# A linear-attention and feed-forward kernel: weights asked for ahead of stores, one visit moved behind two inner products, and banks marked without a full fill

## The chip, the cores and the metric

The kernel runs on one core of a Trainium2 chip. The metric is the time of one execution on the device in microseconds (us), taken over several runs. A core has five engines with instruction queues of their own: PE (matrix products, its weight loads shown apart as PEld), DVE (vector work), ACT (copies and activation functions), POOL (a second, slower vector engine) and SP, which here issues the transfers (DMA). PE writes into eight PSUM banks of 128 partitions by 512 fp32 columns; DVE and ACT read them. Each engine takes its own instructions in order and waits for others by semaphores.

## The reference

Two blocks, one after the other, in fp32. The first is a recurrence with decay for each of 4 sequences and 8 heads of width 64, over 768 steps:

```
state = gamma * state + k[t] (outer) v[t]
y[t]  = scale * q[t] @ state
```

Its outputs, as 3072 tokens of 512, go through a feed-forward block with a leaky function between:

```
h = x @ w_in                 # 512 -> 2048
out = maximum(0.01*h, h) @ w_out   # 2048 -> 512
```

## The kernel before, in words

**Chunks and visits.** The 768 steps are cut into 6 chunks of 128 (`c` from 0 to 5). A chunk of all four sequences (`b` from 0 to 3) is 512 tokens. What the kernel does for a chunk's recurrence is called a *visit*, two sequences at a time. It has products of queries and state (`reads`, line 190), products of masked scores and values (`last_values` L225, `first_values` L214), the sums for the next state (`state`, L240), and ahead of these the *scores* (`scores_to`, L157), products of keys and queries, which DVE multiplies by a causal mask (`masked_apart`, L323) into `am`. DVE then takes the tokens into `x` (`tokens_taken`, L270 and L273) and updates the states (L283, L287). `between`, a tiny POOL instruction (L194), only keeps an order among PE's products. POOL also multiplies the values of coming chunks by their decay (`decay_v`, L127), when they have been loaded (`ahead` L111, `load_kv` L307).

**Feed-forward in units.** The width of 2048 is cut into four units (`u`). For a chunk and a unit there is a hidden product and an output product. Both use Strassen's scheme in Winograd's form: 2 by 2 blocks, seven products M1 to M7 in place of eight, paid for by sums and differences on DVE (`differences`, L489; `plus`, L486). `seven` (L542) issues the seven products into four banks called A, B, C and D. Some banks are shared: M1 is copied by ACT from one bank to another (L635), and a later product is added by PE on top of the copy.

**The first part** does chunks 0 and 1, unit by unit, while the weights arrive. Dictionaries named `hidden_more` and `output_more` say what other work is put after which of the seven products: `s2` means after the third. In the output of chunk 0 and unit 3, written `(0, 3)`, a visit of chunk 2 stands at `s2`, and at `s3` the differences for the last output of chunk 1, those of chunk 2, and the loads of the heads of chunk 3. Sums of the hidden weights are kept in DRAM (`keep_unit`, L909: `kept<-w`, `kept<-sums`).

**The second part** does chunks 2 to 5, 16 units numbered `n`. Here the hidden product has two levels of the scheme. Its weights are streamed from `kept` for each unit by `load_unit`: group 0 into `wa` (L1012, L1013), group 1 into `wb` (L1015, L1016). `inner(n, group)` (L1046) makes the seven inner products of the group into banks 0 to 3: 28 in number times the blocks of the group, four for group 0 and three for group 1, 128 columns each. M1 is copied by ACT into bank 3 (L1050), and M6 is added there without the start flag[...]. ACT copies M5, M4, M6 and M2 out (L1052 to L1058), DVE adds M3 and M7. `outer(n, group)` then adds the inner results to `g` on DVE, and ACT applies the leaky function (L1081). For a unit the order on PE is inner of the next unit's group 0, four products of the output, inner of group 1, three products.

**The seam.** Between the parts the last output of chunk 1 (`last`) is issued in pieces, and between these stand the scores of chunk 3 for sequences 0 and 1, `inner(0, 0)`, the first `joint_visit` of chunk 3 and `inner(0, 1)`. `joint_visit` uses banks 4 to 7 for its sums, and banks 0 to 3 for the scores of the visit that follows. With `scores_first` it computes and masks those scores before its own work. The scores are written with the start flag in each product[...]; `fill(3)` (L575) writes all 512 columns of bank 3 with a product of bf16 values[...], and ACT's copy overwrites the values. It can be issued only after DVE has read the masked scores from the bank.

SP takes the issues of transfers in the order of the program. The order of the last statements before the loop is:

```
for group in range(2):
    load_unit(0, group)
...
inner(0, 0)
outer(0, 0)
products(last, 2)
xs[3] = new_x(3)
joint_visit(3, 0, (3, 2), scores_first=True)
fill(3)
inner(0, 1)
outer(0, 1)
```

Of the kernel before, what the change touches and what calls it, by code (L numbers as in the profile page):

```python
# [9 lines left out]
FP32 = mybir.dt.float32  # L10
# [8 lines left out]
C = 128  # L19
# [3 lines left out]
def kernel(  # L23
# [14 lines left out]
    nc = tc.nc  # L38
# [107 lines left out]

    NS = HP // 2 * 3 * C // 2

    def scores_to(x, ps):
        for m in range(HP // 2):  # L150
            for i in range(2):
                for late in range(2):
                    for j in range(2):
                        s, a = i ^ j, 2 * m + i
                        to = (ps[j][ts(1 - s, 64), m, 1 + s] if late else
                              ps[j][ts(s, 64), m, 0 : 2 + s : 1 + s])
                        nc.tensor.matmul(to, lhsT=x[ts(j, 64), 1, a, ts(late, 64)],  # L157
                                         rhs=x[ts(j, 64), 0, a, late * 64 :])

    turn = [0]  # L160

# [148 lines left out]

    def score_apart(c, b, banks=None):

        if banks is None:
            banks = [ffs.tile([128, HP * C], FP32, tag="ff", bufs=4, name=f"ap{j}_{c}_{b}")
                     for j in range(2)]
        banks = [ps[:, 0:NS] for ps in banks]
        scores[c, b] = [ps.rearrange("p (m n t) -> p m n t", n=3, t=C // 2) for ps in banks]
        scores_to(heads[c, b][0], scores[c, b])

    def masked_apart(c, b, j):  # L320
        if j == 0:
# [11 lines left out]
    def visit(c, b):  # L333

        for f in (reads, last_values, state, first_values):
            for i in range(2):
                f(c, b + i)
        for i in range(2):
            tokens_taken(c, b + i, xs[c][0])
        for i in range(2):  # L340
            state_taken(c, b + i, for_state(sums_at[c, b + i]))
        for i in range(2):
            heads.pop((c, b + i))

    def joint_visit(c, b, following, scores_first=False):

        both = [(c, b), (c, b + 1)]
        later = [(following[0], following[1] + i) for i in range(2)] if following else []
        for i, at in enumerate(both):
            sums_at[at] = [bank[4 + 2 * i + j].rearrange("p (a t) -> p a t", t=C)  # L350
                           for j in range(2)]
        for i, at in enumerate(later) if scores_first else ():
            score_apart(*at, banks=bank[2 * i : 2 * i + 2])
            for j in range(2):
                masked_apart(*at, j)
        for at in both:
            reads(*at)
        for at in both:
            last_values(*at)
        if c < NC - 1:  # L360
            for at in both:
                state(*at)
        else:
            for i in range(2):
                fill(4 + 2 * i, 2, start=False)
        for at in both:
            first_values(*at)
        for i, at in enumerate(later) if not scores_first else ():
            score_apart(*at, banks=bank[2 * i : 2 * i + 2])
        for j in (1, 0):  # L370
            for at in both:
                tokens_taken(*at, xs[c][0], j)
                if j == 0:
                    state_added(*at, for_state(sums_at[at]))
                    heads.pop(at)
        for at in later if not scores_first else ():
            for j in range(2):
                masked_apart(*at, j)
        for at in both:
            state_decayed(*at)  # L380
        for i in range(2):
            ahead(c + 1, b + i)
        for at in later:
            load_kv(*at)
        for at in later:
            decay_v(*at)
# [533 lines left out]
    def sums(c, group):  # L920
        return lambda: sums_of_x(c, group)

    def next_heads():
        for b in range(2):
            ahead(3, b)
            load_kv(3, b)
        for b in range(2):
            decay_v(3, b)
# [17 lines left out]
        (1, 1): dict(s6=[sum_of_unit(1, 1)]),  # L946
        (0, 2): dict(s2=[sum_of_unit(2, 1)], s5=[sum_of_unit(2, 2)]),
        (1, 2): dict(s0=[sum_of_unit(2, 3)], s1=[keep_unit(2)]),
        (0, 3): dict(s2=[lambda: visit(2, 0)],
                     s3=[lambda: differences(*parts[1][1:]), differ(2), next_heads],  # L950
                     s6=[sums(2, 0)]),
    }

# [21 lines left out]
    for u in range(NU):  # L975
# [7 lines left out]
        for c in range(2 if u < NU - 1 else 1):  # L983
            if u == 0:
# [6 lines left out]
    banks = ctx.enter_context(tc.tile_pool(name="banks", bufs=1, space=bass.MemoryType.PSUM))  # L991
    bank = [ffs.tile([128, 4 * C], FP32, tag="ff", bufs=4, name=f"bank{i}") for i in range(4)]
    bank += [banks.tile([128, 4 * C], FP32, name=f"bank{i}") for i in range(4, 8)]
    wa = work.tile([128, 7, 4, C], FP32, tag="late4", name="wa")
    wb_room = work.tile([128, 28 * C], FP32, tag="late6", name="wb")
    wb = wb_room[:, 0 : 21 * C].rearrange("p (j i n) -> p j i n", j=7, i=3)
    made_room = work.tile([128, 28, C], FP32, tag="late0", name="made")
    made_of = [made_room[:, 0:16].rearrange("p (q i) n -> p q i n", q=4),
               made_room[:, 16:28].rearrange("p (q i) n -> p q i n", q=4)]

    N2 = (NC - 2) * NU

    def at_of(n):
        return 2 + n // NU, n % NU

    def load_unit(n, group):

        if n >= N2:
            return
        u = at_of(n)[1]  # L1010
        if group == 0:
            nc.sync.dma_start(out=wa[:, :, 0:1], in_=kept[u][:, :, 0:1])  # L1012
            nc.sync.dma_start(out=wa[:, :, 1:4], in_=kept[u][:, :, 3:6])  # L1013
        else:
            nc.sync.dma_start(out=wb[:, :, 0:2], in_=kept[u][:, :, 1:3])  # L1015
            nc.sync.dma_start(out=wb[:, :, 2:3], in_=kept[u][:, :, 6:7])  # L1016

    def operands(c, group):

# [17 lines left out]
    def inner(n, group, held=False):  # L1037

        c, u = at_of(n)
        w, count = ((wa, 4), (wb, 3))[group]  # L1040
        moving = operands(c, group)
        sums = made_of[group]
        ps = [part[:, 0 : count * C].rearrange("p (i n) -> p i n", n=C) for part in bank[0:4]]
        for m, q, j, s in INNER:
            for i in range(count):
                nc.tensor.matmul(ps[q][:, i], lhsT=w[:, j, i], rhs=part_of(moving[i], s),  # L1046
                                 start=(i == 0 and m in ("M1", "M5", "M4")), stop=True,
                                 skip_group_check=True)
            if m == "M1":
                nc.scalar.copy(out=ps[3], in_=ps[0])  # L1050
            elif m == "M5":
                nc.scalar.copy(out=sums[:, 3], in_=ps[1])  # L1052
            elif m == "M4":
                nc.scalar.copy(out=sums[:, 2], in_=ps[2])
            elif m == "M6":
                nc.scalar.copy(out=sums[:, 1], in_=ps[3])
            elif m == "M2":
                nc.scalar.copy(out=sums[:, 0], in_=ps[0])  # L1058
            elif m == "M3":
                plus(sums[:, 1], sums[:, 1], ps[1])  # L1060
            elif m == "M7":
                plus(sums[:, 3], sums[:, 3], ps[3])
                plus(sums[:, 2], sums[:, 2], ps[3])
        if not held:
            load_unit(n + 1, group)
# [43 lines left out]
    last_room = dict(zip("ABD", map(halves, (0, 3, 2))))  # L1109
    last_room["C"] = [bank[i][:, 0 : z - a] for i, (_, a, z) in zip((1, 5, 4), PIECES)]  # L1110

    for group in range(2):
        load_unit(0, group)
    for i in (4, 6):
        fill(i)
    last = output(1, os[1], [parts[1]], False, True, room=room, order=FUSED)
# [6 lines left out]
        ahead(3, 2 + b)  # L1123
    products(last, 2)
    sums_of_x(2, 1)
    fill(3)
    inner(0, 0)
    outer(0, 0)
    products(last, 2)
    xs[3] = new_x(3)  # L1130
    joint_visit(3, 0, (3, 2), scores_first=True)
    fill(3)
    inner(0, 1)
    outer(0, 1)

    for n in range(N2):
        c, u = at_of(n)
        more = n + 1 < N2
        if u == 0:
            os[c] = new_o(c)  # L1140
        if n + 1 < N2:
            differences(*gs[n][1:])
            if u == NU - 1:
                sums_of_x(c + 1, 1)
        visiting = c + 1 < NC and (u == 1 or u == 0 and n > 0)
        if n + 1 < N2:
            inner(n + 1, 0, held=visiting)
            outer(n + 1, 0)
        if visiting and u == 0:
            xs[c + 1] = new_x(c + 1)  # L1150
            joint_visit(c + 1, 0, (c + 1, 2))
        elif visiting:
            joint_visit(c + 1, 2, (c + 2, 0) if c + 2 < NC else None)
        if visiting:
            load_unit(n + 2, 0)
        steps = output(c, os[c], [gs.pop(n)], u == 0, u == NU - 1, room=room if more else last_room,
                       order=FUSED if more else LAST)
        products(steps, 4)
        if visiting:
            fill(3)  # L1160
        if c + 1 < NC and u == 1:
            differences(*xs[c + 1])
        if c + 1 < NC and u == 2:
            sums_of_x(c + 1, 0)
        if more:
            inner(n + 1, 1)
            products(steps, 1)
            outer(n + 1, 1)
        if n + 2 == N2:
            differences(*gs[n + 1][1:])  # L1170
        products(steps, 3)
# [85 lines left out]
```

## Time and profile before

| What | Value |
|---|---|
| time, median of 3 runs | 658.86 us (657.59 to 660.35) |
| span of the profiled execution | 657.8 us |
| busy: PE, PEld, DVE, ACT, POOL | 639.6, 576.0, 468.2, 263.7, 22.4 us |
| mean granted clock of PE | 0.996 |
| moved by DMA | 113.36 MB |
| PE busy from 200 to 235 us | 34.55 of 35 us |
| PE busy from 235 to 275 us | 30.67 of 40 us |
| PE busy from 275 to 636 us | 360.14 of 361 us |

The page gives the span in 40 slices of 16.4 us, with a digit for the busy share of each engine in tenths. A row of the timeline gives the start, the duration, the engine, the line, what is written and read, the shape, the number of instructions, and in brackets how long the engine stood idle before it and which instruction ended that. Ends of products are modelled, so that two products in a row overlap by some 0.2 us in the rows. The windows of the trace add the granted clock of PE, where 1.00 is full speed.

### The profile page before, as it was taken

Reading aid. Unit: us, or ns where it says so; the run is one execution under the profiler, and the core shown is the slowest. Engines: PE = TensorE matmul, PEld = TensorE weight load, DVE = VectorE, ACT = ScalarE, POOL = GpSimd, SP = SyncE. Lnnn points to the kernel's source line nnn. Section 1 sums busy time; section 2 is a strip of 40 time slices with the busy share of each in tenths; the row PEclk is TensorE's granted clock in tenths of the full one; section 3 lists DMA queues with packets and bytes.
Section 4 is the critical chain, followed back from the end, with each engine's and each line's share of the span. In section 5 each row is a group of like instructions: output and inputs, shape, how many; then the busy total and the mean of one; then the engine's idle time right before and its main releaser. Section 6 shows DMA issues by size and latency. Waiting matters only on the chain.

```text
span 657.8 us, 13283 instructions
## 1 busy us (share of the span) xinstructions
PE 639.6 (97%) x5583; PEld 576.0 (88%) x5583; DVE 468.2 (71%) x782; ACT 263.7 (40%) x495; POOL 22.4 (3%) x45
## 2 busy tenths in 40 slices
PE   8999999999999968899999999999999999999997
PEld 5888888888888858798999999999998999999996
DVE  5789779889979765656876848778637578637655
ACT  5855565265262011450433333323423243433421
POOL 1000000000011100101000010100010000000000
PEclk9999999999999989999999999999999999999999
DMA  8922319365937498547363574636455334545201
GB/s 333 405 100 65 96 65 285 104 231 161 323 157 249 141 313 295 176 125 238 92 192 129 174 246 161 202 114 195 149 177 158 119 116 146 195 127 187 85 0 66
DMA packets 87533, 113.36 MB, mean 172 GB/s; under 512 B 3240, under 2 KB 71720, under 8 KB 87472
## 3 DMA queue, kind: packets, MB, share of 16 engines
q1 hardware_dynamic: 87312, 111.95, 51.7%
q8 instruction: 44, 0.72, 0.5%
q10 hardware_dynamic: 160, 0.55, 0.2%
q14 instruction: 17, 0.14, 0.1%
HBM read 93.35 MB, written 19.14 MB: 171 GB/s over the span
## 4 chain that ended last, share of the span: by engine, by line
PE 93%; DVE 4%; DMA 2%; issue 1%; SPq 0%; ACT 0%; DVEq 0%
PE bank L542 30%; PE bank L1046 27%; PE C_h L542 4%; PE A_h L542 4%; PE B_h L542 4%; PE B_o L542 3%; PE A_o L542 3%; PE C_o L542 3%; PE d L563 2%; PE D_h L542 2%; PE D_o L542 2%; DMA wa<-kept 1%; PE ap L157 1%; PE bank L157 1%; PE bank L225 1%; PE bank L190 1%
## 5 line engine op out<-in xcount | busy, mean ns | idle before, releaser
L486 DVE TENSOR_TENSOR made<-made,bank 128x512 f32<-128x512 f32 (+1 forms) x96 | 56.4, 618 | 77.9 <-PE bank L1046 67.1
L486 DVE TENSOR_TENSOR o<-o,bank 128x512 f32<-128x512 f32 (+2 forms) x91 | 58.5, 661 | 52.1 <-PE bank L542 32.2
L542 PE MATMUL bank<-g,w 128*128 128x256 f32 x384 | 89.3, 381 | 0.3 <-DVE x L270 0.3
L1046 PEld LDWEIGHTS bank<-x,wb 128*128 128x128 f32 x672 | 77.5, 192 | 3.1 <-issue 1.8
L542 PEld LDWEIGHTS bank<-g,w 128*128 128x128 f32 x384 | 71.1, 190 | 9.5 <-DVE x L270 0.5
L1046 PE MATMUL bank<-x,wb 128*128 128x128 f32 x672 | 77.6, 275 | 0.0
L1046 PE MATMUL bank<-x,wa 128*128 128x128 f32 x512 | 70.4, 280 | 3.8 <-ACT bank L1050 2.9
L1046 PEld LDWEIGHTS bank<-x,wa 128*128 128x128 f32 x512 | 65.2, 196 | 6.0 <-ACT bank L1050 3.9
L542 PE MATMUL bank<-gd,w 128*128 128x256 f32 x288 | 66.1, 379 | 0.0
L542 PEld LDWEIGHTS bank<-gd,w 128*128 128x128 f32 x288 | 54.7, 190 | 7.4
L1046 PE MATMUL bank<-t,wa 128*128 128x128 f32 x384 | 53.7, 276 | 3.2 <-DMA wa<-kept 3.2
L1081 ACT ACTIVATE g<-g 128x512 f32<-128x512 f32 x64 | 39.5, 631 | 34.2 <-DVE g L486 34.2
L1046 PEld LDWEIGHTS bank<-t,wa 128*128 128x128 f32 x384 | 48.2, 193 | 3.4 <-DMA wa<-kept 3.4
L1050 ACT COPY bank<-bank 128x512 f32<-128x512 f32 (+1 forms) x32 | 16.8, 523 | 77.5 <-PE bank L1046 77.3
L635 ACT COPY bank<-bank 128x512 f32<-128x512 f32 x17 | 9.7, 571 | 84.6 <-PE bank L542 68.2
L486 DVE TENSOR_TENSOR g<-made 128x512 f32<-128x512 f32 x64 | 42.7, 688 | 1.2
L489 DVE TENSOR_TENSOR gd<-g,gd 128x512 f32<-128x512 f32 x48 | 33.9, 707 | 4.8
L542 PE MATMUL bank<-g,last 128*128 128x256 f32 x120 | 28.4, 381 | 0.9 <-DVE o L486 0.9
L653 ACT COPY bank<-bank 128x512 f32<-128x512 f32 x16 | 9.1, 571 | 48.0 <-PE bank L542 48.0
L542 PE MATMUL bank<-gd,last 128*128 128x256 f32 (+1 forms) x124 | 27.5, 373 | 0.0
L542 PE MATMUL A_h<-x,w 128*128 128x256 f32 x112 | 26.6, 380 | 0.0
L542 PEld LDWEIGHTS bank<-g,last 128*128 128x128 f32 x120 | 22.2, 190 | 4.1 <-DVE o L486 1.3
(182 smaller groups left out, 1031.9 us busy)
## 6 DMA issues: line engine op xcount, KB each, us to landing
wa<-kept SPq DMA_DIRECT2D x16, 1344.0 KB, 7.2
raw<-in_weights_dram SPq DMA_DIRECT2D x31, 512.0 KB, 4.4
wb<-kept SPq DMA_DIRECT2D x16, 896.0 KB, 5.4
kv<-in_kv_dram SPq DMA_DIRECT2D x15, 512.0 KB, 5.3
wa<-kept SPq DMA_DIRECT2D x16, 448.0 KB, 4.1
wb<-kept SPq DMA_DIRECT2D x16, 448.0 KB, 6.3
out_dram<-o SPq DMA_DIRECT2D x23, 256.0 KB, 2.9
kept<-w SPq DMA_DIRECT2D x12, 448.0 KB, 5.6
```

The lines of the kernel that those rows point to most:

```text
L157: nc.tensor.matmul(to, lhsT=x[ts(j, 64), 1, a, ts(late, 64)], rhs=x[ts(j, 64), 0, a, late * 64 :])
L190: mm = nc.tensor.matmul(ps[j][ts(i, 64), m, :], lhsT=st[b][ts(j, 64), a, :], rhs=x[ts(j, 64), 0, a, :], start=(m == 0), stop=False, skip_g ...
L225: nc.tensor.matmul(ps[j][ts(i, 64), m, 64:], lhsT=y[:, 1, 2 * a + j, :], rhs=am[:, j, m, 1 + (i ^ j)], start=(c == 0 and m == 0), stop=Tru ...
L486: nc.vector.tensor_tensor(out=out, in0=a, in1=b, op=ALU.add)
L489: nc.vector.tensor_tensor(out=out, in0=a, in1=b, op=ALU.subtract)
L542: nc.tensor.matmul(to, lhsT=block(w, sa)[:, k, ts(i, 128)], rhs=rhs[:, k, a:z], start=(first and (i == 0 or split) and n == 0 and k == 0), ...
L563: nc.tensor.matmul(banks[r][:, i, :], lhsT=block(2 * u, r + 2 * kh)[:, k, ts(i, 128)], rhs=x[:, 2 * kh + th, k, :], start=(step == 0 and i ...
L635: nc.scalar.copy(out=bank_of("B"), in_=ps)
L653: nc.scalar.copy(out=bank_of("D"), in_=ps)
L1046: nc.tensor.matmul(ps[q][:, i], lhsT=w[:, j, i], rhs=part_of(moving[i], s), start=(i == 0 and m in ("M1", "M5", "M4")), stop=True, skip_gr ...
L1050: nc.scalar.copy(out=ps[3], in_=ps[0])
L1081: nc.scalar.activation(g[:, i], g[:, i], AF.Prelu, alpha=0.01)
```

## The change

There are four parts.

1. The weights of the first unit of the second part (`load_unit(0, 0)` and `load_unit(0, 1)`) are asked for after the first product of the output `(0, 3)`, in `begin_units`, so that they stand in SP's queue ahead of the stores of that output. Before, they stood behind them. The tiles `wa` and `wb` are made there.
2. The differences for the last output of chunk 1 move from `s3` to `s1` of the same output, ahead of the visit.
3. The first joint visit of chunk 3 moves behind `inner(0, 1)` and `outer(0, 1)`. Its scores for the next visit come after its own products, as in the other visits, and their masks come on DVE ahead of the tokens (`masks_first`).
4. `fill(3)` is dropped at the seam and in the loop. Scores that are written into banks 0 to 3 set the start flag only in the first products (`a == 0`)[...], and the columns behind the scores (384 to 511) are marked by a product of 128 columns without the start flag (`tail`). Nothing that DVE reads is in these columns.

```diff
-    def scores_to(x, ps):
+    def scores_to(x, ps, once=False):
...
-                                         rhs=x[ts(j, 64), 0, a, late * 64 :])
+                                         rhs=x[ts(j, 64), 0, a, late * 64 :],
+                                         start=(not once or a == 0), stop=True,
+                                         skip_group_check=True)
...
     def score_apart(c, b, banks=None):
 
+        tail = None
         if banks is None:
...
+        else:
+            tail = banks[1][:, NS:]
         banks = [ps[:, 0:NS] for ps in banks]
...
-        scores_to(heads[c, b][0], scores[c, b])
+        scores_to(heads[c, b][0], scores[c, b], tail is not None)
+        if tail is not None:
+            fill_bank(tail.unsqueeze(1), start=False)
...
-    def joint_visit(c, b, following, scores_first=False):
+    def joint_visit(c, b, following, masks_first=False):
...
-        for i, at in enumerate(later) if scores_first else ():
-            score_apart(*at, banks=bank[2 * i : 2 * i + 2])
-            for j in range(2):
-                masked_apart(*at, j)
...
-        for i, at in enumerate(later) if not scores_first else ():
+        for i, at in enumerate(later):
             score_apart(*at, banks=bank[2 * i : 2 * i + 2])
+        for at in later if masks_first else ():
+            for j in range(2):
+                masked_apart(*at, j)
...
-        for at in later if not scores_first else ():
+        for at in later if not masks_first else ():
...
+    def begin_units():
+
+        streamed.append(work.tile([128, 7, 4, C], FP32, tag="late4", name="wa"))
+        load_unit(0, 0)
+        flat = work.tile([128, 28 * C], FP32, tag="late6", name="wb")
+        streamed.append(flat[:, 0 : 21 * C].rearrange("p (j i n) -> p j i n", j=7, i=3))
+        load_unit(0, 1)
...
-        (0, 3): dict(s2=[lambda: visit(2, 0)],
-                     s3=[lambda: differences(*parts[1][1:]), differ(2), next_heads],
+        (0, 3): dict(s0=[begin_units], s1=[lambda: differences(*parts[1][1:])],
+                     s2=[lambda: visit(2, 0)], s3=[differ(2), next_heads],
                      s6=[sums(2, 0)]),
...
-    for group in range(2):
-        load_unit(0, group)
...
-    fill(3)
     inner(0, 0)
     outer(0, 0)
     products(last, 2)
-    xs[3] = new_x(3)
-    joint_visit(3, 0, (3, 2), scores_first=True)
-    fill(3)
     inner(0, 1)
     outer(0, 1)
+    xs[3] = new_x(3)
+    joint_visit(3, 0, (3, 2), masks_first=True)
...
-        if visiting:
-            fill(3)
```

More of the change, by code (lines that the diff above doesn't have):

```diff
@@ L921, in sums, with at_of, load_unit @@
         return lambda: sums_of_x(c, group)
+    streamed = []
+    N2 = (NC - 2) * NU
+    def at_of(n):
+        return 2 + n // NU, n % NU
+    def load_unit(n, group):
+        if n >= N2:
+            return
+        u = at_of(n)[1]
+        if group == 0:
+            wa = streamed[0]
+            nc.sync.dma_start(out=wa[:, :, 0:1], in_=kept[u][:, :, 0:1])
+            nc.sync.dma_start(out=wa[:, :, 1:4], in_=kept[u][:, :, 3:6])
+        else:
+            wb = streamed[1]
+            nc.sync.dma_start(out=wb[:, :, 0:2], in_=kept[u][:, :, 1:3])
+            nc.sync.dma_start(out=wb[:, :, 2:3], in_=kept[u][:, :, 6:7])
+    def begin_units():
[4 more added lines that the diff above has]
+        load_unit(0, 1)
     def next_heads():
@@ L993 @@
     bank += [banks.tile([128, 4 * C], FP32, name=f"bank{i}") for i in range(4, 8)]
-    wa = work.tile([128, 7, 4, C], FP32, tag="late4", name="wa")
-    wb_room = work.tile([128, 28 * C], FP32, tag="late6", name="wb")
-    wb = wb_room[:, 0 : 21 * C].rearrange("p (j i n) -> p j i n", j=7, i=3)
     made_room = work.tile([128, 28, C], FP32, tag="late0", name="made")
@@ L999 @@
                made_room[:, 16:28].rearrange("p (q i) n -> p q i n", q=4)]
[L1001 to L1016, printed above, removed]
     def operands(c, group):
@@ L1039, in inner @@
         c, u = at_of(n)
-        w, count = ((wa, 4), (wb, 3))[group]
+        w, count = streamed[group], 4 - group
         moving = operands(c, group)
@@ L1140 @@
             os[c] = new_o(c)
+        visiting = c + 1 < NC and (u == 1 or u == 0 and n > 0)
         if n + 1 < N2:
             differences(*gs[n][1:])
-            if u == NU - 1:
-                sums_of_x(c + 1, 1)
-        visiting = c + 1 < NC and (u == 1 or u == 0 and n > 0)
+        if n + 1 < N2 and u == NU - 1:
+            sums_of_x(c + 1, 1)
         if n + 1 < N2:
```

## The prediction

> **What bounds the kernel now.** I read the page first, then the chain of waits between 197 and 290 us, then the timeline of PE, SP and DVE there, then the granted clock in short windows.
>
> ```profile
> PE 639.6 (97%) x5583; PEld 576.0 (88%) x5583; DVE 468.2 (71%) x782; ACT 263.7 (40%) x495; POOL 22.4 (3%) x45
> ...
> PE   8999999999999968899999999999999999999997
> ```
>
> PE (matrix products) is busy 97% of the span, so only what stops PE or adds to it counts. The row of 40 slices (16.4 us each) has one dip outside the ends: the fifteenth to the seventeenth digit (6, 8, 8), 230 to 280 us. That is where the change works: the seam between the first two chunks and the second part. PE's timeline there (start, duration, instruction; in brackets the idle time before it and what ended it):
>
> ```profile
> 231.15 1.57 PE L157 MATMUL bank<-qk 64*64 64x128 f32 x64
> 232.65 1.99 PE L542 MATMUL bank<-g,last 128*128 128x256 f32 x8
> 235.50 1.99 PE L542 MATMUL bank<-g,last 128*128 128x256 f32 x8 [0.86 <-DVE o L486]
> 237.36 0.38 PE L575 MATMUL bank<-mask 128*128 128x512 bf16 x1
> 238.59 0.49 PE L1046 MATMUL bank<-x,wa 128*128 128x128 f32 x2 [0.86 <-DMA wa<-kept]
> 242.31 1.22 PE L1046 MATMUL bank<-t,wa 128*128 128x128 f32 x6 [3.23 <-DMA wa<-kept]
> ...
> 260.54 0.38 PE L575 MATMUL bank<-mask 128*128 128x512 bf16 x1 [1.84 <-DVE am L323]
> ...
> 271.19 1.38 PE L1046 MATMUL bank<-x,wa 128*128 128x128 f32 x10 [2.91 <-ACT bank L1050]
> ```
>
> Five stops: 0.86 + 0.86 + 3.23 + 1.84 + 2.91 = 9.70 us. In the 361 us from 275 to 636 PE is busy 360.1, so nothing else of this kind is left there. The third stop has a consequence, seen in the windows (stretch, its length, busy time of the engines; then the granted clock and the DMA):
>
> ```profile
> 242.00:244.00 2.00, 1.69 (x10) 1.69 (x11) 0.00 (x0) 0.44 (x1) 0.00 (x0) 0.70 1.15 323
> 244.00:246.00 2.00, 2.00 (x11) 2.00 (x11) 0.00 (x0) 0.72 (x2) 0.00 (x0) 0.50 1.10 375
> 246.00:248.00 2.00, 2.00 (x19) 2.00 (x19) 0.00 (x0) 0.94 (x2) 0.00 (x0) 0.94 1.02 399
> ```
>
> Full speed less the granted clock over these windows is 0.60 + 1.00 + 0.12 = 1.72 us lost. Why were the weights late? SP's queue (starts of the DMA issues):
>
> ```profile
> 206.18 4.19 SPq L909 DMA_DIRECT2D kept<-w  x3
> 215.48 0.34 SPq L111 DMA_DIRECT2D qk<-in_qk_dram  x1
> ...
> 229.30 3.72 SPq L622 DMA_DIRECT2D out_dram<-o  x4
> 233.07 0.61 SPq L1012 DMA_DIRECT2D wa<-kept  x1
> 233.74 0.70 SPq L1013 DMA_DIRECT2D wa<-kept  x1
> ```
>
> The weights' issues stand behind four stores whose data DVE finishes at 228.6 to 231; the second one takes from 233.74 to about 242.27 to land. And DVE is the cause of the stores' lateness: it is 9.83 us busy of the 10 from 220 to 230. The last stop is a chain of three engines:
>
> ```profile
> 268.69 0.70 DVE g L486
> 269.39 0.02 issue
> 269.42 1.23 ACT g L1081 x2
> 270.65 0.49 ACT bank L1050
> ```
>
> inner(0,1) is followed at once by inner(1,0), so the sums of `outer` (DVE to 269.98), two leaky functions and only then the copy into bank 3 (ACT works in order) stand before M6.
>
> [...] 3.23 us of idle, 0.86 before it, then clock 0.50 at its lowest; the 2.91 us stop drew no loss (1.00 in 271 to 275). [...] That is what the fill of bank 3 is for; in the trace it is a 0.38 us row that spaces its neighbours by 0.21 (311.22 to 311.43) and that waited 1.84 for the masks at 260.54. [...]
>
> **The change part by part.**
>
> *Weights of unit 0 asked for in the output of chunk 0.* Four issues move from 233 to right behind the stores into `kept` (last issue ends at 210.4). `wa` takes the room of the sums stored by `kept<-sums` (first issues at 202.2, landing 4.7 us), `wb` that of w6, which `kept<-w` reads (about 7 us to landing: 214 to 216). So `wa` is asked for at about 211 and `wb` at 215. 1792 + 1344 KB are 3.2 MB, 9 us at the 355 GB/s of 240 to 242: all there by about 224. Needed at 236 and 246. The 0.86 and 3.23 us stops and the 1.72 us of clock go. Behind SP's wait stand the heads of chunk 3, which themselves wait for PE until 215.48 and 218.4: one more microsecond there. [...]2.1 MB of heads come behind the weights: 6 us, done at 228 to 230; scores need qk at 231.15. Hidden, with two to four us to spare.
>
> *differences(parts[1]) moved ahead of the visit.* 3.37 us of DVE (221.72 to 225.09; 2.89 in the same four at 269.90) go to 213.8, where DVE has gaps of 1.11 and 2.71 before the yp row of L214 releases it at 218.33. Its operands are there (ACT's leaky ends at 211.4). o[1] comes 2.3 us later there, at 217.2; its bank B is written next at 223.7. All DVE work after 221.7 comes some 3 us earlier: the add that M7 waited for ends at about 232 to 233 instead of 235.4, ahead of the 234.4 at which PE wants it. The first 0.86 goes. Two decays on POOL slow single DVE rows (x L489 1.53 against 0.68); they move by some us and cost the same, inside this slack.
>
> *The visit behind both inner products.* Its own work (reads, values, state: 3.5 us; scores 1.5) is unchanged. inner(0,1) no longer stands behind the masks, and its fill goes: the 1.84 stop goes. Between inner(0,1) and inner(1,0) there are now 5.1 us of visit, which cover the chain DVE to ACT of the last stop: that 2.91 goes too. In its place comes a new wait: the masks of the next scores. DVE ends the sums of outer(0,1) 4.4 us after PE ends inner(0,1) (269.98 less 265.62), then needs 1.96 for four masks, then ACT 0.57 to copy into bank 3: 6.9 us. PE reaches M6 after 5.1 of visit and 1.35 of M1, M5, M4: 6.45. New wait: 0.45 us (between 0 and 1.5, if POOL slows DVE). Tokens, states and differences come after the masks on DVE, about 2.7 + 2.9 us, hidden by the 6.25 of inner(1,0); the first product of the output that needs a difference starts 1.7 later still.
>
> *Fills.* Seven fills of bank 3 go (two at the seam, five in the visits of the loop), 0.21 each. Twelve of 128 columns come. No row shows these: a quarter of 0.21 is 0.055 at the least; the 0.10 of the fill's weight load is the most. I take 0.06. Start flags of the scores change no count or duration.
>
> **The sum.** PE from 231.15, each stretch with its steady duration: scores 1.50 and tails 0.12 (232.8), M2 1.93 and M7 1.73 (236.4), inner(0,0) 6.25 (242.7), M3 and M4 3.46 (246.1), inner(0,1) 4.69 (250.8), visit 3.5 and scores 1.5 with tails 0.12 (256.0), inner(1,0) 6.25, 0.2 of transitions and the new wait 0.45 (262.8). Before, this point is at 275.03: 12.2 us. Counter-check by causes: 9.70 + 1.72 + 0.42 fills - 0.24 tails - 0.45 wait = 11.2, and every stop also ends a run of pipelined matmuls, whose last one shows some 0.2 us of drain: five times 0.2 makes 12.2. In the loop five fills less eight tails: 1.05 - 0.48 = 0.6. In all 12.8: 658.86 - 12.8 = 646.1 us.
>
> **The rivals.**
>
> *The masks, or the heads' late transfers, take part of it back.* For it: POOL's decays and the heads fall at other times, and 2 to 4 us of slack in DMA and 1.5 in DVE are thin. Against: DVE has idle time everywhere around. A stop of 3 us at the scores or at M6, without a loss of clock: 649.5 us. Chance 0.17.
>
> *The early loads don't take effect* (their room comes free late[...], so that they land at 240 again). Then only the visit's part is left: 1.84 + 2.91 + drains 0.4 + fills 0.8 - 0.45 = 5.5, and the DVE part 0.9: 652.5 us. Against: `kept<-w` lands by 216. Chance 0.07.
>
> *Slower: weights ahead of the heads hold PE up at the scores.* From 202 on 3.2 MB of stores into `kept`, 3.2 of weights and 2.1 of heads are 8.5 MB; at 190 GB/s, as in 210 to 220, they end at 247, 15.5 us after the scores want them: 658.86 - 12.8 + 15.5 = 661.6 us. Against: 273 GB/s from 200 to 210 while stores ran, and the low share later is want of requests. Chance 0.03.
>
> *More than expected*: no wait at M6, tails free: 645.2 us. Chance 0.10, the forecast 0.63.
>
> **How the numbers follow.** 646.1 us is the likeliest. The range: low is the better case less the 1.3 us by which single runs lie under the median (657.59 against 658.86), 643.8; high takes in the first rival, 650.0; what lies outside are the other two and some of the noise. Faster by over 0.5% (under 655.6) are all cases but the slow one, less something for a wait that I don't see: 0.93; same 0.04; slower 0.03.
>
> **What would show it.** Right: `wa<-kept` issued near 211; no PE idle with DMA `wa<-kept`; clock 1.0 throughout 230 to 260; output(2,0) starting near 263; no row of L575 with 512 columns after the visits; PE idle between 0 and 1.5 us before M6 of inner(1,0), ended by ACT and behind it `am`. Wrong: PE idle at the scores of chunk 3 ended by DMA `qk`; `wa` issued after 220; a new stop at M7 or M6 over 2 us.

## The result, and the profile after

The changed kernel takes 649.42 us (median of 3 runs, 647.93 to 650.44) against 658.86 before: a ratio of 0.9853, with a 95% interval of 0.9808 to 0.9899. The span of the profiled execution fell from 657.8 to 647.7 us. So the change is faster by 9.4 us, where 12.8 was forecast.

The page of the changed kernel, the lines that answer to those shown of before:

```profile
PE 638.0 (99%) x5588; PEld 575.2 (89%) x5588; DVE 467.8 (72%) x782; ACT 263.9 (41%) x495; POOL 22.1 (3%) x45
...
PE   8999999999999998999999999999999999999997
```

The dip of three slices has become one digit, 8, at 243 to 259 us. Line numbers moved: L1046 is now L1060, L542 is L548, L575 is L581, L323 is L330. PE's timeline in the seam:

```profile
232.31 3.67 PE L548 MATMUL bank<-g,last 128*128 128x256 f32 x16
235.82 0.38 PE L1060 MATMUL bank<-x,wa 128*128 128x128 f32 x2
...
245.53 4.85 PE L1060 MATMUL bank<-x,wb 128*128 128x128 f32 x42
250.31 1.10 PE L192 MATMUL bank<-qk,states 64*64 64x128 f32 x32
...
255.72 0.44 PE L1060 MATMUL bank<-x,wa 128*128 128x128 f32 x2
256.00 0.72 PE L1060 MATMUL bank<-t,wa 128*128 128x128 f32 x5
258.55 0.38 PE L1060 MATMUL bank<-t,wa 128*128 128x128 f32 x1 [1.83 <-issue]
```

All five stops of the seam are gone. One is new: 1.83 us in `inner(1,0)`, and no engine and no transfer is named for it ("issue": PE waited for nothing that the profile shows). It stands between two products of one group, the seventh and the eighth, with the same operands, so it isn't the wait for the masks at M6 that was forecast. The masks did take their time, and lie under it:

```profile
254.80 2.01 DVE L330 TENSOR_TENSOR am<-bank,mask 128x384 f32<-128x384 f32 x4
...
258.97 0.57 ACT L1064 COPY bank<-bank 128x512 f32<-128x512 f32 x1 [3.53 <-PE bank L1060]
```

The masks end at 256.8; ACT's copy into bank 3, free from then on, waits for PE until 258.97. SP's queue, and the windows over the stretch in which the clock had fallen to 0.50 before:

```profile
210.17 1.41 SPq L942 DMA_DIRECT2D wa<-kept  x1
211.63 1.50 SPq L943 DMA_DIRECT2D wa<-kept  x1
215.00 0.52 SPq L946 DMA_DIRECT2D wb<-kept  x1
...
224.35 2.21 SPq L628 DMA_DIRECT2D out_dram<-o  x4
```

```profile
242.00:244.00 2.00, 2.00 (x12) 1.79 (x11) 1.75 (x4) 0.00 (x0) 0.00 (x0) 1.00 0.33 77
244.00:246.00 2.00, 2.00 (x13) 1.80 (x12) 1.92 (x4) 0.00 (x0) 0.00 (x0) 1.00 1.05 336
```

The weights are asked for at 210 and 215, the stores come at 224, and the clock is 1.00.

Where the time went, between the two profiled executions. By the rows of the timeline, the stretch from the first score of chunk 3 to the first product of output(2,0) was 231.15 to 274.86 us, 43.7 us, and is 230.42 to 264.12, 33.7 us: 10.0 gained, of 12.2 forecast. (In the chain of waits, whose times are used below, that product starts at 275.03 and at 264.29.) From there to the last sum of the kernel the chain takes 376.8 us before (275.03 to 651.84) and 377.5 now (264.29 to 641.79): 0.7 lost, where a gain of 0.6 was forecast. And the scores of chunk 3 start 0.7 us earlier. That isn't a gain of the change: the profile of before has a stop near its start, in a part of the program that is the same in both, which the other profile hasn't, and from there on the changed kernel is 0.7 ahead.

```profile
23.79 0.46 PE L214 MATMUL yp<-am,in 64*64 64x64 f32 x14 [0.61 <-issue]
```

The experiments look for the two differences from the forecast, and for what each part is worth.

### The profile page after: what moved, and what is told of

It reads as the page before. It is cut to its first block, busy times and chain, and to the rows that moved or that the text cites. A ratio compares the mean times of both kernels' runs of the same rounds, so it can differ in the third digit from the quotient of the medians.

```text
span 647.7 us, 13304 instructions
## 1 busy us (share of the span) xinstructions
PE 638.0 (99%) x5588; PEld 575.2 (89%) x5588; DVE 467.8 (72%) x782; ACT 263.9 (41%) x495; POOL 22.1 (3%) x45
## 4 chain that ended last, share of the span: by engine, by line
PE 97%; DMA 1%; DVE 1%; issue 1%; DVEq 0%
PE bank L548 32%; PE bank L1060 27%; PE B_o L548 4%; PE C_h L548 4%; PE A_o L548 4%; PE A_h L548 4%; PE B_h L548 4%; PE C_o L548 4%; PE d L569 2%; PE D_o L548 2%; PE D_h L548 2%; PE bank L157 1%; PE ap L157 1%; PE bank L227 1%; PE bank L192 1%; PE yp L227 1%
## 5 line engine op out<-in xcount | busy, mean ns | idle before, releaser
L548 PE MATMUL bank<-g,w 128*128 128x256 f32 x384 | 89.1, 380 | 0.3 <-DVE x L272 0.3
L548 PEld LDWEIGHTS bank<-g,w 128*128 128x128 f32 x384 | 71.2, 190 | 9.1 <-DVE x L272 0.5
L1060 PEld LDWEIGHTS bank<-x,wb 128*128 128x128 f32 x672 | 77.6, 192 | 0.8
L1060 PE MATMUL bank<-x,wb 128*128 128x128 f32 x672 | 77.6, 275 | 0.0
L1060 PE MATMUL bank<-x,wa 128*128 128x128 f32 x512 | 68.7, 276 | 0.0
L548 PE MATMUL bank<-gd,w 128*128 128x256 f32 x288 | 66.1, 379 | 0.0
L1060 PEld LDWEIGHTS bank<-x,wa 128*128 128x128 f32 x512 | 63.8, 192 | 1.6 <-ACT bank L1064 0.8
L548 PEld LDWEIGHTS bank<-gd,w 128*128 128x128 f32 x288 | 54.7, 190 | 7.4
L1060 PE MATMUL bank<-t,wa 128*128 128x128 f32 x384 | 53.6, 275 | 1.8 <-issue 1.8
L1060 PEld LDWEIGHTS bank<-t,wa 128*128 128x128 f32 x384 | 48.1, 192 | 2.0 <-issue 2.0
L548 PE MATMUL bank<-g,last 128*128 128x256 f32 x120 | 28.1, 380 | 0.0
L548 PE MATMUL bank<-gd,last 128*128 128x256 f32 (+1 forms) x124 | 27.5, 373 | 0.0
L548 PE MATMUL A_h<-x,w 128*128 128x256 f32 x112 | 26.6, 380 | 0.0
L548 PEld LDWEIGHTS bank<-gd,last 128*128 128x128 f32 x124 | 22.9, 190 | 3.3 <-DVE gd L495 0.3
```

The costliest lines, as they stand in the source:

```text
L548: nc.tensor.matmul(to, lhsT=block(w, sa)[:, k, ts(i, 128)], rhs=rhs[:, k, a:z], start=(first and (i == 0 or split) and n == 0 and k == 0), ...
```

## The experiments

All are edits of the changed kernel. All but the last were timed beside the kernel before, and the ratios are to that kernel. They ran in three groups of four, the second of them on another chip. The unaltered changed kernel is in the first group only, so the runs of the other two are set against it by their ratios, and their order among themselves is mostly inside the noise; what the parts cost is read from the rows.

**The changed kernel again** (no edit).

> The changed kernel unaltered, beside the variants, so that they have it on the same chip. 649.4 us as measured, within 1.5; its profile should show PE stop once, 1.8 us in inner(1,0) with nothing named as the cause. If that stop is chance, it is gone or elsewhere here; if it belongs to the program (place in the instruction stream and transfers under way), it stands at the same product.

Measured: 650.41 us, ratio 0.986 (0.9819 to 0.9901). The stop is at the same product (258.74, 1.82 us), so it belongs to the program. In this execution it cost more than itself: the windows behind it show the granted clock (before the DMA share) at half.

```profile
258.00:260.00 2.00, 1.26 (x9) 1.26 (x10) 2.00 (x6) 0.57 (x1) 0.00 (x0) 0.88 1.05 409
260.00:262.00 2.00, 2.00 (x11) 2.00 (x11) 1.79 (x4) 0.59 (x1) 0.00 (x0) 0.50 0.81 318
```

Output(2,0) starts at 266.11 here, 1.6 us later after the scores of chunk 3 than in the first profile. So the stop costs 1.8 us in some executions and some 3.4 in others. The profile of the run with tails in bank 3 only (below) shows the same: a stop of 1.96, then a clock of 0.50 from 260 to 262.

**Weights asked for behind the stores again, differences early.**

```diff
-        (0, 3): dict(s0=[begin_units], s1=[lambda: differences(*parts[1][1:])],
+        (0, 3): dict(s1=[lambda: differences(*parts[1][1:])],
...
+    begin_units()
     for i in (4, 6):
         fill(i)
```

> The changed kernel with the unit's weights asked for behind the stores again; the differences stay early. Theory 1: the stores were late because DVE was late, and with the differences early they are issued at 224 to 226.6; the weights follow at 226.6, the second tile lands some 9.2 us later as before, at 235.8, and PE wants it at 236.0. Then almost nothing is lost: 0 to 1 us, 649.4 to 650.5. Theory 2: the place in the queue is what counts, and the two stops (0.86 and 3.23) and the clock loss (1.72) come back: 654 to 656.

Measured: 651.65 us, 1.2 more than the changed kernel beside it; the intervals of the two ratios overlap (0.9841 to 0.9925 here), and its profile is 0.7 behind at output(2,0). Theory 1 holds. SP's queue of this kernel, and PE's only stop on a transfer:

```profile
225.00 2.12 SPq L628 DMA_DIRECT2D out_dram<-o  x4
227.17 0.61 SPq L942 DMA_DIRECT2D wa<-kept  x1
227.84 0.69 SPq L943 DMA_DIRECT2D wa<-kept  x1
```

```profile
235.74 0.39 PE L1060 MATMUL bank<-x,wa 128*128 128x128 f32 x2
236.55 0.94 PE L1060 MATMUL bank<-t,wa 128*128 128x128 f32 x6 [0.42 <-DMA wa<-kept]
```

With the differences early the stores go at 225 in place of 229.3, and weights that stand behind them land 0.4 us too late, not 4.

**Differences behind the visit again, weights early.**

```diff
-        (0, 3): dict(s0=[begin_units], s1=[lambda: differences(*parts[1][1:])],
-                     s2=[lambda: visit(2, 0)], s3=[differ(2), next_heads],
+        (0, 3): dict(s0=[begin_units],
+                     s2=[lambda: visit(2, 0)],
+                     s3=[lambda: differences(*parts[1][1:]), differ(2), next_heads],
```

> The changed kernel with the four differences behind the visit again; the weights stay early. Theory 1: only the stop of M7 comes back, 0.9 us with its drain: 650.3. Theory 2: DVE's sums for inner(0,0), masks and stores come 3 us later too and hold PE at the inner products: 2 to 4 us, 651.5 to 653.5. Theory 3: hidden, 649.4.

Measured: 649.96 us, no difference, and no stop at M7: theory 3. In this profile PE is 0.4 us earlier at the scores, but the stop in `inner(1,0)` is longer and ends at the same time as in the changed kernel, so that nothing is left of it:

```profile
258.59 0.38 PE L1061 MATMUL bank<-t,wa 128*128 128x128 f32 x2 [2.38 <-issue]
```

The sum that M7 needs ends at 233.5; PE wants it at 233.7, so that it is just in time. In the kernel before it ended at 235.4, and part of that was POOL: its two decays at 222.0 and 226.8 stretched two DVE groups (2.14 against 1.42 for the pair of differences, 1.53 against 0.68 for the last one of `x`). With the weights ahead of the heads the decays come at 227.3 and 229.8, and stretch one group by 0.8.

**Both undone**: the two edits above together. Only the visit's place and the tails stay changed.

> The changed kernel with both the unit's weights behind the stores and the differences behind the visit, as before; only the visit's place and the tails stay changed. Taken alone, the one cost 1.2 us and the other nothing. Theory 1: the two parts cover the same stops, each alone is enough, and without both the stops of 0.86, 0.86 and 3.23, the clock loss of 1.72 and their drains come back: +6 to +7, 656 to 657. Theory 2: they are independent: +1, 651.

Measured: 656.51 us, ratio 0.9955 (0.9935 to 0.9975). Theory 1 holds: the stops are back, with a clock of 0.88 over 236 to 250 as before.

```profile
235.07 2.00 PE L548 MATMUL bank<-g,last 128*128 128x256 f32 x8 [0.51 <-DVE o L492]
237.98 0.46 PE L1060 MATMUL bank<-x,wa 128*128 128x128 f32 x2 [0.91 <-DMA wa<-kept]
241.61 1.45 PE L1060 MATMUL bank<-t,wa 128*128 128x128 f32 x6 [3.17 <-DMA wa<-kept]
```

Together the two parts are worth 6 to 7 us; leaving out either loses 1.2 or nothing.

**The visit between the two inner products again**, with scores first and tails in place of fills.

```diff
...
+    xs[3] = new_x(3)
+    joint_visit(3, 0, (3, 2), scores_first=True)
     inner(0, 1)
     outer(0, 1)
-    xs[3] = new_x(3)
-    joint_visit(3, 0, (3, 2), masks_first=True)
```

> The changed kernel with the first joint visit between the two inner products again, scores first, with the tails in place of the fills; weights and differences stay early. Theory 1, as predicted: the stops of 1.84 and 2.91 come back in about that size, less the 1.8 us stop in inner(1,0) if that belongs to the visit's place: plus 3 to 5 us, 652.5 to 654.5. Theory 2: the 1.84 was the fill's alone; without it M1, M5 and M4 run while the masks are read, and the stop is under 1 us; only the 2.91 comes back: plus 1 to 3 us, 650.5 to 652.5.

Measured: 654.04 us, 3.6 more than the changed kernel beside it, in theory 1's range, but not by its stops (line numbers are 4 higher here):

```profile
251.68 4.96 PE L1064 MATMUL bank<-x,wb 128*128 128x128 f32 x42 [0.45 <-DVE am L330]
...
263.50 1.78 PE L1064 MATMUL bank<-x,wa 128*128 128x128 f32 x7 [4.19 <-ACT bank L1068]
```

Without the fill the wait for the masks is 0.45 in place of 1.84 (theory 2 was right there), and the chain DVE to ACT waits longer, 4.19 in place of 2.91. The 1.3 us more are two sums of `outer` on DVE, 0.69 each in the kernel before, beside which POOL's decays run here:

```profile
257.33 1.04 POOL L127 TENSOR_TENSOR kv<-kv,dec 128x512 f32<-128x512 f32 x1 [8.49 <-DMA kv<-in_kv_dram]
257.80 1.12 DVE L496 TENSOR_TENSOR g<-made 128x512 f32<-128x512 f32 x1
258.59 1.23 POOL L127 TENSOR_TENSOR kv<-kv,dec 128x512 f32<-128x512 f32 x1 [0.22 <-DMA kv<-in_kv_dram]
258.85 1.52 DVE L496 TENSOR_TENSOR g<-g,made 128x512 f32<-128x512 f32 x1
```

Around the stop the clock is 0.98 over 230 to 265 and 0.97 over 265 to 300, some 1.5 us lost. Against these stands the stop of 1.83 in `inner(1,0)`, which this kernel doesn't have. The chain is what the move of the visit covers.

**Full fills in place of tails.**

```diff
-            tail = banks[1][:, NS:]
+            tail = None
...
+    fill(3)
     inner(0, 0)
...
     joint_visit(3, 0, (3, 2), masks_first=True)
+    fill(3)
...
         products(steps, 4)
+        if visiting:
+            fill(3)
```

> The changed kernel with full fills of bank 3 (512 columns, behind the masks) in place of the tails. The fill behind the first visit waits for the masks, which end 1.4 us after PE's scores. Theory 1: a tail costs 0.17 as its neighbours' spacing shows[...]: plus 1.4, plus 7 fills by 0.21, less 12 tails by 0.17: +0.9, 650.3. Theory 2: a tail costs 0.06 as predicted, and the loop's extra time is something else: +2.2, 651.6. Either can be shifted by up to 1.8 if the unexplained stop of PE goes elsewhere.

Measured: 648.44 us, ratio 0.9828 (0.9797 to 0.9858): not slower than the changed kernel, and both theories missed the likeliest value.

```profile
256.86 0.38 PE L581 MATMUL bank<-mask 128*128 128x512 bf16 x1 [1.41 <-DVE am L330]
...
258.68 2.94 PE L1060 MATMUL bank<-x,wa 128*128 128x128 f32 x24 [0.34 <-issue]
```

The fill waits for the masks by 1.41, as expected, and the stop of PE behind it shrinks to 0.34: 1.75 in all, and PE is at the same point as with the tails (output(2,0) at 264.08 against 264.29). The two waits lie over one another. The rest of the kernel takes 376.9 us, against 377.5 with tails; about half of these 0.6 us are the tails, the rest is a stop without a named cause, 0.82 with tails (at 397.69) and 0.27 here.

**Tails in bank 3 only.** M5 begins bank 1 with the start flag; no tail stands behind its scores here.

```diff
-            tail = banks[1][:, NS:]
+            tail = banks[1][:, NS:] if banks[1] is bank[3] else None
```

> The changed kernel with tails in bank 3 only: bank 1 is begun with the start flag by M5 of each inner product[...]. Six tails fewer, those that stand between two sequences' scores. Theory 1 (0.17 each): minus 1.0, 648.4. Theory 2 (0.06 each): minus 0.4, 649.0.

Measured: 648.75 us, ratio 0.9833 (0.9793 to 0.9874); in medians nearer to theory 2, but the rows show that both prices are true, in different places. First the scores of chunk 3 in the changed kernel, then here:

```profile
230.42 0.90 PE L157 MATMUL bank<-qk 64*64 64x128 f32 x32
231.25 0.23 PE L581 MATMUL bank<-mask 128*128 128x128 bf16 x1
231.41 0.90 PE L157 MATMUL bank<-qk 64*64 64x128 f32 x32
232.25 0.23 PE L581 MATMUL bank<-mask 128*128 128x128 bf16 x1
232.31 3.67 PE L548 MATMUL bank<-g,last 128*128 128x256 f32 x16
```

```profile
230.53 1.57 PE L157 MATMUL bank<-qk 64*64 64x128 f32 x64
232.04 0.23 PE L581 MATMUL bank<-mask 128*128 128x128 bf16 x1
232.10 3.67 PE L548 MATMUL bank<-g,last 128*128 128x256 f32 x16
```

From the first score to M2 it is 1.89 with two tails, 1.57 with one, and 1.50 with none (230.60 to 232.10, full fills). So the tail at the end costs 0.07, and the one between the scores 0.32. The products around that one are on tiles of 64 by 64, the tail itself on 128 by 128; the tail at the end stands where the tile size changes anyway. Both tails change the type from fp32 to bf16 and back, so the type alone doesn't make the difference; no run separates the tile size from the rest.

**Loads of the heads later**: the loads and decays at the end of the first joint visit move behind `inner(1,0)`.

```diff
+        def rest():
             for i in range(2):
                 ahead(c + 1, b + i)
...
+        if hold:
+            return rest
+        rest()
...
             outer(n + 1, 0)
+        if n == 0:
+            held_rest()
```

> The changed kernel with the loads and decays at the end of the first joint visit put behind inner(1,0) and outer(1,0), so that few transfers run while PE is in the visit and the first products of inner(1,0). Theory 1: the 1.83 us stop in inner(1,0) is PE waiting for its next instructions, whose fetch goes through the same engines as 3 MB of loads and shares them: it falls under 0.5 us, 647.5 to 648. Theory 2: the fetch takes as long in any case, because the visit's small products use instructions up faster than they come: 1.8 us stays, 649.4. Theory 3: it is a wait for a semaphore that the profile doesn't show, on the masks: 0.5 to 1.8 stays and ACT or DVE is named.

Measured: 649.66 us, ratio 0.9846 (0.9812 to 0.9879). Theory 2:

```profile
258.17 0.38 PE L1065 MATMUL bank<-t,wa 128*128 128x128 f32 x1 [1.56 <-issue]
```

```profile
256.00:258.00 2.00, 0.61 (x6) 0.42 (x4) 2.00 (x7) 0.00 (x0) 0.00 (x0) 1.00 0.21 55
```

The DMA share is 0.21 in this window, where it was 1.03 in the changed kernel, and the stop is 1.56 in place of 1.83. Traffic is not what makes it.

**One tail and later heads together.**

> One tail and the heads' loads later, together, as a candidate. If both theories 1 hold: minus 1.0 and minus 1.5, 646.9. If neither: 649.

Measured: 647.93 us, ratio 0.9828 (0.9795 to 0.9861), with the stop at 1.85. Between the two cases of its expectation; its distance from later heads alone (649.66) lies inside the intervals.

**Scores behind `inner(1,0)`.**

```diff
...
-    joint_visit(3, 0, (3, 2), masks_first=True)
+    scores_of_next = joint_visit(3, 0, (3, 2), scores_later=True)
...
             outer(n + 1, 0)
+        if n == 0:
+            scores_of_next()
```

> The changed kernel with the scores and masks for the visit after the first one put behind inner(1,0) and outer(1,0), where the loop's other visits have them: 132 small PE instructions fewer in a row before inner(1,0). Theory 1: the 1.8 us stop is PE waiting for its next 256 instructions, which the dense visit uses up faster than they are fetched; with scores later it falls away or comes as under 0.5 us, and what is left at M6 is ACT's copy behind the leaky functions, about 0.6 us: minus 0.8 to 1.4 in the seam, 648 to 649.5. Theory 2: the stop is a hidden wait of inner(1,0) for DVE or for its weights: it stays at 1.5 to 2 us.

Measured: 648.44 us, ratio 0.9824 (0.9792 to 0.9857). The stop is gone, as theory 1 has it, and the wait at M6 that it left open didn't show either:

```profile
254.21 0.49 PE L1069 MATMUL bank<-x,wa 128*128 128x128 f32 x2
254.54 0.83 PE L1069 MATMUL bank<-t,wa 128*128 128x128 f32 x6
255.21 3.07 PE L1069 MATMUL bank<-x,wa 128*128 128x128 f32 x26
```

Both sides of M6 lie in one unbroken row of 26. From the first score of chunk 3 to output(2,0) it is 32.6 us by the chain, 1.2 less than in the changed kernel, though the scores take 2.5 us in their new place where they took 1.8.

**The same with tails in bank 3 only.**

> The same with tails in bank 3 only. Minus 0.5 to 1.0 against scores_after in the profile, from six places without a change of tile size between two sequences' scores; 647.5 to 648.5. A candidate for the best version.

Measured: 647.37 us (646.02 to 647.83), ratio 0.9809 (0.9776 to 0.9841), the lowest median of all, by less than the intervals. In the two profiles there is no difference to see (spans 645.9 and 646.1): in this one PE has stops of 0.9, 0.6 and 0.3 without a named cause elsewhere, which the other one hasn't, and which take up what the tails give.

**PE's instructions moved on by 180.** 90 small products that compute nothing are put at the start.

```diff
     keep_busy(10)
+    for _ in range(90):
+        nc.tensor.matmul(idle[:, 0, 0:32], lhsT=nothing, rhs=nothing[:, 0:32], start=True, stop=True,
+                         skip_group_check=True)
```

> The changed kernel with 90 small bf16 products (weight load and 32 columns each) at the start, which do nothing but move all later PE instructions on by 180. They cost up to 10 us at the start, so only the seam is compared, not the time. Theory 1: the stop stands at a fixed count of PE instructions[...], not at a product. It leaves inner(1,0) and comes 180 instructions earlier in the program, about 4.5 us before the end of the scores, where the slow products of inner(0,1) have given the fetch more time: 0.2 to 1.0 us. Theory 2: it belongs to inner(1,0): 1.8 us at the same product.

Measured in one profiled execution: the scores of chunk 3 start 2.1 us later than in the changed kernel, and output(2,0) at the same time, 264.29. The seam has no stop:

```profile
257.76 0.23 PE L581 MATMUL bank<-mask 128*128 128x128 bf16 x1
257.82 0.44 PE L1063 MATMUL bank<-x,wa 128*128 128x128 f32 x2
258.10 0.83 PE L1063 MATMUL bank<-t,wa 128*128 128x128 f32 x6
258.77 3.07 PE L1063 MATMUL bank<-x,wa 128*128 128x128 f32 x26
```

Nothing in the seam itself was edited. So the stop depends on how many instructions PE has had, not on the product. One of its kind comes in a place where the changed kernel has none:

```profile
368.85 1.24 PE L548 MATMUL bank<-g,w 128*128 128x256 f32 x5 [0.41 <-issue]
```

A count in the traces (products, weight loads and PE's waits for semaphores) says the same. In the changed kernel the stops without a named cause come after 4801, 5569 and 7617 PE instructions (1.83, 0.11 and 0.82 us); these differ by 3 and 8 times 256. The stop in `inner(1,0)` comes after 4801 in all nine profiles that have it (in the one with the weights behind the stores the profile names DVE at it, at the same count). The stop of the shifted kernel at 368.85 comes after 7105, which is 9 times 256 more than 4801, though its product is another. The kernel before has two of them as well, the one at 23.79 after 705 and this one in the loop after 5569:

```profile
303.73 0.55 PE L157 MATMUL bank<-qk 64*64 64x64 f32 x11 [0.50 <-issue]
```

The page has the transfers that bring instructions:

```profile
q8 instruction: 44, 0.72, 0.5%
```

44 packets of 16 KB for the 11,264 PE instructions in the trace (5,588 products, as many weight loads, and 88 others) are 256 in each, if all of them are PE's (an estimate: the page doesn't say whose they are). None of these stops comes where 256 instructions last 8 us and more, as in most of the loop; in the changed kernel they come where a visit uses 256 up in 3.4 to 4.2. The packet before the stop in `inner(1,0)` starts at 255.97 in the trace, lasts 1.2, and PE goes on at 258.55. At all five stops of this kind in the traces of the two kernels (23.79 and 303.73 before, 258.55, 292.80 and 397.69 now) PE goes on 1.3 to 1.5 us after the end of the last packet, whether the stop is 0.11 or 1.83 us long. So the counts and the packets point to PE waiting for its next instructions; no view names it. What sets the packet's start is open: 256 instructions of the changed kernel, up to 366.78, went in 3.35 us without a stop, and the stop after 7617 is between 0.27 and 1.40 us in ten of the profiles and missing in the others.

## Why the prediction was right, and by its steps

The measured 649.42 us lies in the range, near its upper end. The room there was made for a rival of another cause, so that part of the hit is luck. The mechanism was right for the weights, the differences and the chain from DVE to ACT; the new wait and the price of the tails were wrong.

*Weights asked for early.* Right: issued at 210 and 215, no stop on `wa`, clock 1.00, no stop on the heads in the seam. The weights landed by 225.8 (forecast 224), and the heads behind them, in the order of their issue, from 227.1 to 230.9 (forecast 228 to 230). What it missed is that this part and the next cover for each other. The prediction saw that DVE made the stores late, but didn't draw the conclusion that curing DVE alone would nearly do: about 1 us was lost without the early weights (0.7 in the profile, 1.2 in medians whose intervals overlap).

*Differences ahead of the visit.* The stop at M7 is gone, but this part alone isn't its cause: it was gone with the differences behind the visit as well (649.96 us), and back with 0.51 when the weights were late too.

*The visit behind both inner products.* Right in direction: the chain DVE to ACT is covered, and the move is worth 3.6 us, in spite of the new stop. The step that failed is "New wait: 0.45 us (between 0 and 1.5, if POOL slows DVE)". The masks take about what was forecast: with a copy of 0.57 behind them it is 7.0 us from the end of `inner(0,1)` (250.4 to 257.4), against 6.9. But PE is at M6 later than was reckoned. "1.35 of M1, M5, M4" is half of what 24 products take in the kernel before (265.6 to 268.3, 2.7 us); with that the sum leaves no wait, and in the shifted kernel, where no other stop hides it, none is seen. The stop of 1.8 us that came is, by the counts and packets above, PE's fetch of instructions. The range for this term was too narrow because it was drawn from engines only. There was a sign: of the 0.86 us that PE is idle from 275 to 636 in the kernel before, passed over as "nothing else of this kind", 0.50 is the stop at 303.73. The 1.84 us of before, booked as removed, hid no fetch: that stop ends after 4695 PE instructions, 106 short of 4801, which PE reaches at 266.4, amid the slower products of `inner(0,1)`, when the packet of 259.06 to 260.5 has long landed. With the visit in its old place and that stop down to 0.45 there is no stop of this kind in the seam either. It was the move that brought 4801 right behind a visit.

*Fills.* The term of the sum that was mis-sized: "Twelve of 128 columns come." at 0.06 each. The six at the end of scores cost 0.07; the six between scores 0.32. In the seam that is 0.5 more than allowed. In the loop PE's lead over the kernel before shrinks by 0.13 at each of the two visits that have no stop in either profile, and grows by 0.22 where a fill alone went: for four visits and that fill 0.3 lost, where 0.6 gained stood. This part of the change brings no time. That bank 3 has to have a fill or a tail at all was the author's reasoning: no run leaves out both.

*The sum.* In the seam, fetch 1.83 for 0.45 (1.4), tails 0.5 and small terms 0.3: 2.2 short. In the loop, tails 0.9, and stops for fetch 0.4 (0.82 and 0.11 now, 0.50 before): 1.3 short. Less the 0.7 of luck ahead of the seam, 2.8: the difference between 12.8 and 10.0 in the profiled executions. The medians show 9.4; that the clock falls behind the stop in some executions is part of that, and only single profiles show it. Two smaller sums don't come out: no wait and free tails give 644.9 from the terms named, not 645.2, and a stop of 3 us gives 649.1, not 649.5. Neither changes the argument.

*The rivals.* The first one (a stop of 3 us, 649.5) came true in its time and not in its cause. Neither the early loads' failure nor a hold-up by the heads was seen.

## What to carry to other kernels

A late transfer that stands behind a store has two cures, an earlier place in the queue and an earlier engine; work out each alone, since here both together gained little more than one. When a stretch of many small instructions is moved, ask what stands behind it: it can outpace the fetch of instructions (here, where 256 of them went in 3.4 to 4.2 us), and then the order in which dense and slow stretches follow one another matters. Look for idle time without a named cause in the profile of before; it was there. A tiny product between others on a different tile size cost over four times what it cost where the size changes anyway; put it there, and only in the bank that needs it.

## What the runs showed of the hardware that was not expected

PE stopped for 0.1 to 2.4 us at counts of instructions that differ by multiples of 256, and the stop in `inner(1,0)` hardly depended on traffic (1.56 us with a DMA share of 0.21, 1.83 with 1.03). A stop of 1.82 us and one of 1.96 each drew the clock to 0.50 for a window, as the 3.23 us in the kernel before had; others of 1.83 and 2.38, and the 2.91 us in the kernel before, drew nothing. What decides it is open. DVE's sums of 128 by 512 took 1.12 and 1.52 us in place of 0.69 beside a decay on POOL. A product of 128 bf16 columns cost 0.32 us between products on 64 by 64 tiles and 0.07 behind them.
